# A gated linear attention and a routed MLP: the attention's instructions put in order by a list of operations with times

## The chip, the core and the metric

One core of a Trainium2 chip runs the program. Its engines work side by side and meet through semaphores: TensorE (PE, matmuls; PEld its weight loads), VectorE (DVE), ScalarE (ACT), GpSimd (POOL), and SyncE (SP), whose queue issues the DMAs here. The metric is the device time of one execution in microseconds; lower is better.

## The reference

The attention is a recurrence over 768 tokens for 4 batches of 8 heads of width 48; its output rows go to a mixture of 8 experts, one expert a row.

```python
mag = np.sqrt(a_re * a_re + a_im * a_im)
scale = np.minimum(mag, 0.999) / (mag + 1e-06)
a_re_n, a_im_n = (a_re * scale, a_im * scale)
...
for t in range(S):
    ar, ai = (a_re_n[:, :, t, :, None], a_im_n[:, :, t, :, None])
    new_re = ar * S_re - ai * S_im
    new_im = ar * S_im + ai * S_re
    kv = np.einsum('bhd,bhe->bhde', k[:, :, t], v[:, :, t])
    S_re, S_im = (new_re + kv, new_im)
    y[:, :, t] = np.einsum('bhd,bhde->bhe', q[:, :, t], S_re)
...
logits = x @ w_gate
expert_idx = np.argmax(logits, axis=1)
...
for e in range(E):
    mask = expert_idx == e
    xe = x[mask]
    h = np.maximum(xe @ w1[e], 0.0)
    ye = h @ w2[e]
    out[mask] = gate_w[mask, None] * ye
```

All inputs are float32: q, k, v and both gate parts are (4, 8, 768, 48); w1 is (8, 384, 1024), w2 (8, 1024, 384).

## The kernel before

The program has three parts in a row: the attention of the four batches, a short routing part, and 31 row tiles of the experts' MLP. The change touches the attention alone.

**What VectorE does for a batch (`front`).** Tokens are cut into 48 blocks of 16, and channels lie on partitions. `limit` turns the raw gates into a scale, in four pieces: per piece ScalarE squares, takes a logarithm, an exponential, a square and one affine pass with a bias held in a tile (`u<-l,w_bias`), and VectorE does four passes over 576 columns (`s<-sq`, `s<-s,u`, `l<-s,l`, `sc<-l,u`). The scaled gates are written into X (`X<-raw,sc`), which holds three parts per position: the negated imaginary part (ScalarE writes it), the real and the imaginary part. A chain over the 15 further positions of a block multiplies the gates up (`z<-X`, 576 columns, then `X<-z`, 288 columns). Small steps of 72 and 36 columns carry the products across blocks (`zc`, `carry`). `fix(t)` then brings the carried products into a third t of the channels (six passes of 672 columns), and `fold(t)` makes q times the product and k over the product (eight passes of 768 columns), into tiles called `pk`. SP ships `pk` to per-head tiles KX and QX by DMAs, for q and k, real and imaginary parts, one per piece of a head. Six KX/QX pairs serve the eight heads of a batch in turn; `pk` has three buffers.

**What the attention does for a group of heads (`attention`).** The groups of a batch have 2, 3 and 3 heads; their tokens come in six chunks of 128. In each chunk TensorE makes scores (`at<-QX,KX`), VectorE masks them (`am<-at,causal`), TensorE adds the masked scores times the values and the state times the queries into `y`, ScalarE moves `y` to `xf`; for the next chunk TensorE makes the turned state (`sp`) and ScalarE copies it to `st`. The scores' matmul is 224 columns wide, since QX holds a rotation matrix beside each chunk's queries: VectorE builds it for five chunks of a head at once (`QX<-diag,KX`, 96x480), and ScalarE copies the turned keys out (`kt<-at`). In the last group of a batch each finished chunk of 128 rows is transposed (`px`), copied (`xt`), multiplied with the gate weights (`lg`) and stored to `x_hbm`.

**What sets the order.** The instructions of VectorE, ScalarE and TensorE keep the order in which the Python code issues them (`InOrder`). `front` and `attention` are generators. `front` yields a guess of VectorE's time after each step; a group's `attention` generator is put on the list `waiting` with a start time (`spent[0] + SHIP`, 4.0), and `heads_until` takes steps from it as long as its own clock `spent[1]` is not ahead of `front`'s. `limit` of the next batch is drawn into the chain one step at a time from the seventh position on. The tiles come from rotating pools.

Of the kernel before, what the change touches and what calls it, by code (L numbers as in the profile page):

```python
# [21 lines left out]
BL = 16  # L22
# [7 lines left out]
SHIP = 4.0  # L30
# [8 lines left out]
def segments(t):  # L39

    r, out = t * 128, []
    while r < t * 128 + 128:
        n = min(D - r % D, t * 128 + 128 - r)
        out.append((r // D, r - t * 128, n, r % D))
        r += n
    return out
# [14 lines left out]
def gateloop_then_moe(ctx, tc, q, k, a_re, a_im, v, wg, w1, w2, out):  # L61
# [60 lines left out]
    with ExitStack() as att:  # L122
        pool = lambda nm, n, **kw: att.enter_context(tc.tile_pool(name=nm, bufs=n, **kw))
        ld = pool("ld", 2)
        one = pool("one", 1)
        two = pool("two", 2)
        sm = pool("sm", 3)
        psA = pool("psA", 4, space=PSUM)
        psY = pool("psY", 1, space=PSUM)
        psS = pool("psS", 1, space=PSUM)  # L130
        psX = pool("psX", 1, space=PSUM)
        psL = pool("psL", 1, space=PSUM)
        V, A, T = (InOrder(tc, e) for e in (nc.vector, nc.scalar, nc.tensor))
# [7 lines left out]


        KXs = [one.tile([128, KW], FP32, name=f"KX{i}") for i in range(RING)]
        QXs = [one.tile([128, C, 256], FP32, name=f"QX{i}") for i in range(RING)]
        KTs = [one.tile([128, 3, 128], FP32, name=f"kt{i}") for i in range(2)]
# [6 lines left out]
        X = one.tile([128, BL, 3, NC], FP32, name="X")  # L152
        xf = one.tile([128, C, DM], FP32, name="xf")
        turn, taken = [0], set()

        def load(b):
            raws = []
            for i in range(BL // JQ):
                js = slice(i * JQ, i * JQ + JQ)
                raw = ld.tile([128, JQ, 2, NC], FP32, name="raw", bufs=BL // JQ)  # L160
                nc.sync.dma_start(raw[:, :, 0, :], a_re[b, :, js, :])
                nc.sync.dma_start(raw[:, :, 1, :], a_im[b, :, js, :])
                raws.append(raw)
            return raws

        def limit(b, raws, scales):

            held, sqs = {}, {}

            def squares(i):  # L170
                if i < BL // JQ:
                    sq = two.tile([128, BL, 2, C * NB], FP32, name="sq").rearrange("p j u n -> p (j u n)")[:, 0:JQ * 2 * NC]
                    sqs[i] = sq.rearrange("p (j u n) -> p j u n", u=2, n=NC)
                    A.activation(sqs[i], raws[i], func=ACT.Square)
            squares(0)
            for i in range(BL // JQ + 2):
                if i < BL // JQ:
                    s = two.tile([128, JQ, NC], FP32, name="s")
                    sq = sqs.pop(i)
                    vstt(s, sq[:, :, 0, :], 1e-12, sq[:, :, 1, :], ALU.max, ALU.add)  # L180
                    yield
                if i >= 2:

                    _, l, u = held.pop(i - 2)
                    sc = two.tile([128, JQ, NC], FP32, name="sc", bufs=BL // JQ)
                    vstt(sc, l, -2 / 0.999, u, ALU.max, ALU.mult)
                    scales.append(sc)
                    yield
                if i < BL // JQ:
                    l, u = (two.tile([128, JQ, NC], FP32, name=x) for x in "lu")  # L190
                    A.activation(l, s, func=ACT.Ln)
                    A.activation(l, l, func=ACT.Exp, scale=-0.5)
                    A.activation(u, l, func=ACT.Square, accum_out=good[:, b, G * C + i:G * C + i + 1])
                    held[i] = s, l, u
                    squares(i + 1)
                if 1 <= i <= BL // JQ:

                    s1, l, u = held[i - 1]
                    vtt(s1, s1, u, ALU.mult)
                    yield  # L200
                    vstt(l, s1, -3.0, l, ALU.add, ALU.mult)
                    A.activation(u, l, func=ACT.Identity, scale=-0.5e-6 * 0.4995, bias=w_bias)
                    yield

        def front(b, raws, scales, heads, ahead):

            for i in range(BL // JQ):
                js = slice(i * JQ, i * JQ + JQ)
                vtt(X[:, js, 1:3, :], raws[i], bc(scales[i][:, :, None, :], [128, JQ, 2, NC]), ALU.mult)
                A.activation(X[:, js, 0, :], X[:, js, 2, :], func=ACT.Copy, scale=-1.0)  # L210
                yield 1.3
            raws[:] = load(b + 1) if b + 1 < B else []
            more = limit(b + 1, raws, ahead) if b + 1 < B else iter(())
            qs, ks = [], []
            for t in range(G):
                for x, src in ((qs, q), (ks, k)):
                    x.append(ld.tile([128, BL, C * NB], FP32, name="qt" if x is qs else "kt_in", bufs=1))
                    nc.sync.dma_start(x[t], src[b, :, t])

            for j in range(1, BL):  # L220
                cur, prev = X[:, j], X[:, j - 1]
                z = two.tile([128, 2, 2, NC], FP32, name="z")
                vtt(z, dims(cur, 0, (NC, 2), (NC, 2), (1, NC)), dims(prev, 2 * NC, (-NC, 2), (0, 2), (1, NC)), ALU.mult)
                if j > 6:
                    next(more, None)
                vtt(cur[:, 1:3, :], z[:, 0], z[:, 1], ALU.add)
                if j > 6:
                    next(more, None)
                yield 2.4 if j > 6 else 1.3
            for _ in more:  # L230
                pass

            last = one.tile([128, 3, NC], FP32, name="last")
            V.tensor_copy(last[:, 1:3, :], X[:, BL - 1, 1:3, :])
            V.tensor_scalar_mul(last[:, 0, :], X[:, BL - 1, 2, :], -1.0)
            carry = one.tile([128, 2, G * C, NB], FP32, name="carry")
            lv = last.rearrange("p u (n b) -> p u n b", b=NB)
            V.tensor_copy(carry[:, :, :, 1], lv[:, 1:3, :, 0])
            yield 0.7
            for n in range(2, NB):  # L240
                z = two.tile([128, 2, 2, G * C], FP32, name="zc")
                vtt(z, dims(last, n - 1, (NC, 2), (NC, 2), (NB, G * C)),
                    dims(carry, NC + n - 1, (-NC, 2), (0, 2), (NB, G * C)), ALU.mult)
                vtt(carry[:, :, :, n], z[:, 0], z[:, 1], ALU.add)
                yield 0.6
            TC = C * NB

            def fix(t):
                ts = slice(t * TC, t * TC + TC)
                xv = X[:, :, :, ts].rearrange("p j u (n b) -> p j u n b", b=NB)[:, :, :, :, 1:]  # L250
                shape = [128, BL, C, NB - 1]
                y = {}
                for x, w, nm in ((0, 0, "s"), (1, 1, "l"), (0, 1, "u"), (1, 0, "u")):
                    y[x, w] = two.tile([128, BL * TC], FP32, name=nm)[:, 0:BL * C * (NB - 1)]
                    y[x, w] = y[x, w].rearrange("p (j n b) -> p j n b", j=BL, b=NB - 1)
                    vtt(y[x, w], xv[:, :, 1 + x], bc(carry[:, w:w + 1, t * C:t * C + C, 1:], shape), ALU.mult)
                    yield 0.77
                vtt(xv[:, :, 1], y[0, 0], y[1, 1], ALU.subtract)
                yield 0.77
                vtt(xv[:, :, 2], y[0, 1], y[1, 0], ALU.add)  # L260
                yield 0.77

            def fold(t):
                ts = slice(t * TC, t * TC + TC)
                sq = two.tile([128, BL, 2, TC], FP32, name="sq")
                s, l = (two.tile([128, BL, TC], FP32, name=x) for x in "sl")
                A.activation(sq, X[:, :, 1:3, ts], func=ACT.Square)
                qp = two.tile([128, 2, KW], FP32, name="pk", bufs=3)
                kp = two.tile([128, 2, KW], FP32, name="pk", bufs=3)
                by_chunk = lambda ap: ap.rearrange("p j (c n) -> p c j n", n=NB)  # L270
                chunks = lambda ap: ap.rearrange("p (c j n) -> p c j n", j=BL, n=NB)
                pu = [by_chunk(X[:, :, 1 + u, ts]) for u in range(2)]
# [158 lines left out]
        def heads_until(now):  # L431
            while waiting and spent[1] <= now:
                ready, gen = waiting[0]
                spent[1] = max(spent[1], ready)
                if spent[1] > now:
                    break
# [320 lines left out]
```

## Time and profile before

| what | us |
|---|---|
| median of 3 runs (lowest, highest) | 882.89 (880.92, 884.51) |
| the profiled execution's own time | 885.0 |
| its span in the trace | 883.3 |
| busy: PE, DVE, ACT, POOL | 621.0, 422.3, 218.3, 138.0 |

The span counts from the first to the last instruction in the trace; stretches below are given in microseconds from its start. The chain that ended last holds only the last stores of the MLP, so it tells nothing of the attention. The attention is therefore read from the busy time of stretches and from the instructions in order of time: the stretches are cut where a batch's first mask (`am`) starts and where its last one starts.

### The profile page before, as it was taken

The page shows a single profiled execution, that of the slowest core. Times are in us where ns is not written, and L with a number is a line of the kernel's source. Part 1 is how long each engine was busy: PE and PEld are TensorE (multiplying, and loading weights), DVE is VectorE, ACT ScalarE, POOL GpSimd, SP SyncE. Part 2 cuts the span into 40 slices and gives each one's busy share as a digit, 9 for nine tenths or more (in the row PEclk, how much of TensorE's full clock was granted, in tenths as well). Part 3 has the DMA queues.
Part 4 walks back from the last instruction along what each step waited for, and adds up shares of the span by engine and source line. Part 5 has one row for each costly group of instructions (what it writes and reads, how often), then busy time and mean ns, then how long its engine had stood idle before and what let it go on. Part 6 is the DMA issues. An engine that isn't in the chain of part 4 may idle for free. (4 is left out here: it accounts for less than half of the span.)

```text
span 883.3 us, 10745 instructions
## 1 busy us (share of the span) xinstructions
PE 621.0 (70%) x3985; PEld 534.7 (61%) x3985; DVE 422.3 (48%) x760; ACT 218.3 (25%) x538; POOL 138.0 (16%) x160
## 2 busy tenths in 40 slices
PE   0000558926689167963599149999999999999997
PEld 0000557925679157962599047777777777777775
DVE  4889767896878958778631521111111111111111
ACT  5462236632356324332333100000000000000000
POOL 6000000000000000000000032333333333333320
PEclk9999978967879677985799659999999999999999
DMA  7302455235532444135221167787888798878850
GB/s 197 107 1 53 121 128 128 71 98 136 132 104 81 118 121 111 37 86 143 68 64 46 12 243 311 315 316 311 343 318 303 300 367 335 306 299 342 315 197 1
DMA packets 67627, 156.47 MB, mean 177 GB/s; under 512 B 9873, under 2 KB 50866, under 8 KB 59634
## 3 DMA queue, kind: packets, MB, share of 16 engines
q0 software_dynamic: 12896, 108.36, 32.0%
q1 hardware_dynamic: 51474, 47.36, 20.4%
q8 instruction: 33, 0.54, 0.2%
q10 hardware_dynamic: 3200, 0.01, 0.2%
q14 instruction: 24, 0.20, 0.1%
HBM read 127.23 MB, written 10.83 MB: 156 GB/s over the span
## 5 line engine op out<-in xcount | busy, mean ns | idle before, releaser
L57 PE MATMUL at<-QX,KX 128*128 128x224 f32 (+1 forms) x384 | 92.3, 382 | 165.9 <-DVE QX L57 165.9
L704 PEld LDWEIGHTS h_ps<-xt,w1t 128*128 128x128 f32 x1488 | 173.5, 194 | 12.7 <-issue 4.8
L57 PEld LDWEIGHTS at<-QX,KX 128*128 128x128 f32 x384 | 73.4, 215 | 171.2 <-issue 98.1
L704 PE MATMUL h_ps<-xt,w1t 128*128 128x128 f32 x1488 | 173.8, 277 | 4.4 <-issue 4.4
L710 PE MATMUL o_ps<-w2t,ht 128*128 128x384 f32 x496 | 167.9, 492 | 8.5 <-ACT ht L706 8.2
L710 PEld LDWEIGHTS o_ps<-w2t,ht 128*128 128x128 f32 x496 | 91.7, 190 | 71.9 <-ACT ht L706 14.4
L57 PE MATMUL y<-vb,am 128*128 128x128 f32 x384 | 78.3, 298 | 42.9 <-ACT xf L57 42.9
L706 ACT ACTIVATE ht<-h_ps 128x512 f32<-128x512 f32 x31 | 18.5, 598 | 357.0 <-PE h_ps L704 357.0
L57 PEld LDWEIGHTS y<-vb,am 128*128 128x128 f32 x384 | 67.1, 212 | 44.6 <-ACT xf L57 44.1
L712 DVE TENSOR_SCALAR yo<-o_ps,xs 128x384 f32<-128x384 f32 x31 | 19.2, 618 | 143.6 <-PE o_ps L710 143.6
L699 DVE COPY xt<-xt_ps 128x384 f32<-128x384 f32 x31 | 17.3, 557 | 139.8 <-PE xt_ps L697 139.8
L474 POOL MEMSET state<- 128x1152 f32 x1 | 1.1, 1063 | 472.6 <-DMA x_hbm<-xf 472.6
L57 PE MATMUL y<-st,QX 128*128 128x128 f32 x320 | 67.4, 294 | 3.4 <-ACT st L57 2.9
L57 DVE TENSOR_TENSOR am<-at,causal 128x256 f32<-128x256 f32 x120 | 41.1, 368 | 52.5 <-PE at L57 52.4
L57 PE MATMUL sp<-vb,kt 128*128 128x128 f32 x320 | 62.0, 288 | 0.0
L713 POOL DMA_INDIRECT out_dram<-yo,idx x31 | 31.5, 1016 | 194.0 <-DVE yo L712 193.1
L57 PEld LDWEIGHTS y<-st,QX 128*128 128x128 f32 x320 | 52.2, 205 | 6.6 <-ACT st L57 6.6
L57 PE MATMUL sp<-st,QX 128*128 128x128 f32 x256 | 52.7, 289 | 0.0
L57 ACT COPY kt<-at 128x192 f32<-128x192 f32 (+1 forms) x100 | 25.5, 288 | 102.3 <-DVE am L57 102.3
L57 PEld LDWEIGHTS sp<-vb,kt 128*128 128x128 f32 x320 | 50.6, 206 | 0.0
L57 DVE TENSOR_TENSOR z<-X 128x576 f32<-128x576 f32 x60 | 45.1, 752 | 0.7
L57 PEld LDWEIGHTS sp<-st,QX 128*128 128x128 f32 x256 | 40.8, 201 | 0.0
(142 smaller groups left out, 718.0 us busy)
## 6 DMA issues: line engine op xcount, KB each, us to landing
KX<-pk SPq DMA_DIRECT2D x48, 146.2 KB, 3.3
QX<-pk SPq DMA_DIRECT2D x48, 144.0 KB, 3.5
raw<-in_a_re_dram SPq DMA_DIRECT2D x16, 288.0 KB, 4.6
raw<-in_a_im_dram SPq DMA_DIRECT2D x16, 288.0 KB, 5.2
qt<-in_q_dram SPq DMA_DIRECT2D x12, 384.0 KB, 3.8
kt_in<-in_k_dram SPq DMA_DIRECT2D x12, 384.0 KB, 3.2
vb<-in_v_dram SPq DMA_DIRECT2D x24, 192.0 KB, 3.0
x_hbm<-xf SPq DMA_DIRECT2D x24, 192.0 KB, 2.7
```

Of the source, the lines that this page charges most:

```text
L57: return lambda *a, **kw: self.tc.keep_in_program_order(f(*a, **kw))
L474: nc.gpsimd.memset(state, 0.0)
L699: nc.vector.tensor_copy(xt, xt_ps)
L704: nc.tensor.matmul(h_ps[:, f, :], lhsT=w1t[:, c:c + 128], rhs=xt[:, d, :], start=(d == 0), stop=(d == DT - 1))
L706: nc.scalar.activation(ht[:, 0:FT // 2, :], h_ps[:, 0:FT // 2, :], func=ACT.Relu)
L710: nc.tensor.matmul(o_ps, lhsT=ht[:, f, :], rhs=w2t[:, f * DM:f * DM + DM], start=(f == 0), stop=(f == FT - 1))
L712: nc.vector.tensor_scalar_mul(y, o_ps, xs[:, DM:W])
L713: nc.gpsimd.indirect_dma_start(out=out[:, :], out_offset=bass.IndirectOffsetOnAxis(ap=idx[:, j:j + 1], axis=0), in_=y, in_offset=None, bou ...
```

## The change

The attention is no longer issued as the code runs. Each step is put on a list as an `Op` with its engine (V, A, T or S for SP), the time that it keeps its engine, the time until others may use its result (`late`), the operations that it needs (`after`), those whose buffer it overwrites (`free`), and a rank (`first`). `in_time` then places the operations one by one at the earliest time of the four engines; among those that are ready on an engine it takes the lowest rank, then the one with the longest way to the end. The instructions are issued in that order, SP's DMAs too.

Beside the order:

- the gates are loaded into four fixed tiles `gate` of three parts and scaled in place; X keeps two parts. ScalarE copies position 0 to X, and makes `last` (VectorE did before);
- the rotation matrices are made by ScalarE, one 96x48 ACTIVATE for each half, chunk and head, with the factor from a column of KX (`diagonal`), where VectorE had one 96x480 pass for a head;
- all tiles of the attention are fixed buffers with their own names instead of pools' turns, and PSUM is eight fixed banks (`bank0` to `bank3` are the scores, then `y`, `sp`, `px`, `lg`);
- `zrow` stands in a small pool of its own, released before the `setup` tiles are made.

```diff
-SHIP = 4.0
...
+class Op:
+    def __init__(self, engine, busy, late, emit, after, free, first):
+        self.engine, self.busy, self.late, self.emit, self.first = engine, busy, late, emit, first
+        self.after, self.free = [o for o in after if o], [o for o in free if o]
+        self.start = None
+    def ready(self):
+        t = 0.0
+        for o in self.after:
+            t = max(t, o.start + o.late)
+        for o in self.free:
+            t = max(t, o.start + (o.busy if o.engine == self.engine else o.late))
+        return t
...
+def in_time(ops):
...
+    while len(out) < len(ops):
+        best = None
+        for e, l in able.items():
+            if l:
+                t = max(clock[e], min(x[0] for x in l))
+                if best is None or t < best[0]:
+                    best = t, e
+        t, e = best
+        r, o = min((x for x in able[e] if x[0] <= t), key=lambda x: (x[1].first, -way[x[1]]))
+        able[e].remove((r, o))
+        o.start, clock[e] = t, t + o.busy
...
-    zrow = consts.tile([1, W], FP32, name="zrow")
-    nc.vector.memset(zrow, 0.0)
-    nc.sync.dma_start(x_hbm[N:N + 1, :], zrow)
+    with tc.tile_pool(name="zero", bufs=1) as setup:
+        zrow = setup.tile([1, W], FP32, name="zrow")
+        nc.vector.memset(zrow, 0.0)
+        nc.sync.dma_start(x_hbm[N:N + 1, :], zrow)
...
+        def dve(cols, emit, after=(), free=(), first=5):
+            return op("V", cols / 960 + 0.068, cols / 960 + 0.19, emit, after, free, first)
+        def act(cols, emit, after=(), free=(), first=5, n=1):
+            return op("A", n * 0.08 + cols / 1200, n * 0.08 + cols / 1200 + 0.15, emit, after, free, first)
+        def pe(passes, emit, after=(), free=(), first=5):
+            return op("T", passes * 0.111, passes * 0.111 + 0.21, emit, after, free, first)
+        def dma(late, emit, after=(), free=()):
+            return op("S", 0.62, late, emit, after, free)
...
-                vtt(X[:, js, 1:3, :], raws[i], bc(scales[i][:, :, None, :], [128, JQ, 2, NC]), ALU.mult)
-                A.activation(X[:, js, 0, :], X[:, js, 2, :], func=ACT.Copy, scale=-1.0)
+                o = dve(2 * n, lambda g=g, s=s: vtt(g[:, :, 1:3, :], g[:, :, 1:3, :], bc(s[:, :, None, :], [128, JQ, 2, NC]), ALU.mult),
+                        [sc])
+                m = act(n, lambda g=g: A.activation(g[:, :, 0, :], g[:, :, 2, :], func=ACT.Copy, scale=-1.0), [o])
...
-            for i in range(n):
-                ends = KX[i][0:R2, S:KW].rearrange("p (c w) -> p c w", w=2)[:, 0:C - 1, :, None]
-                shape = [R2, C - 1, 2, D]
-                vtt(QX[i][0:R2, 0:C - 1, 128:128 + R2].rearrange("p c (w d) -> p c w d", w=2),
-                    bc(diag[:, None, :, :], shape), bc(ends, shape), ALU.mult)
+            for c in range(C - 1):
+                for i in range(n):
+                    def diagonal(i=i, c=c):
+                        for w in range(2):
+                            A.activation(QX[i][0:R2, c, 128 + w * D:128 + w * D + D], diag[:, w, :], func=ACT.Copy,
+                                         scale=KX[i][0:R2, S + 2 * c + w:S + 2 * c + w + 1])
+                    turn[c, i] = act(96, diagonal, kd[i], state.get(("head", slots[i]), []), first=2, n=2)
...
-        for b in range(B):
-            heads, ahead = {}, []
-            for x in front(b, raws, scales, heads, ahead):
-                if isinstance(x, tuple):
-                    waiting.append((spent[0] + SHIP, attention(b, x[0], heads)))
-                else:
-                    spent[0] += x
-                heads_until(spent[0])
+        load_gates(0)
+        limit(0)
+        for b in range(B):
+            front(b)
+            if b + 1 < B:
+                load_gates(b + 1)
+            fixed = [fix(t) for t in range(G)]
+            for t in range(G):
+                fold(b, t, fixed[t])
+                attention(b, t)
+            if b + 1 < B:
+                limit(b + 1)
+        for o in in_time(ops):
+            o.emit()
```

What moves, at three places. First VectorE, in the first batch, from the masks of the first group's third chunk on (`am` masks, `pk<-X,qt` and `pk<-X,l` or `pk<-X,fl` the products with q and k, `s`, `l` or `fs`, `fl` steps of `fold`). Before:

```order
L57 TENSOR_TENSOR am<-at,causal 128x256
L57 TENSOR_TENSOR pk<-X,l 128x768 x2
L57 TENSOR_TENSOR pk<-X,qt 128x768
L57 TENSOR_TENSOR am<-at,causal 128x256
L57 SCALAR_TENSOR_TENSOR s<-sq 128x768
L57 TENSOR_TENSOR pk<-X,qt 128x768
L57 TENSOR_SCALAR good<-s 128x6
L57 TENSOR_TENSOR am<-at,causal 128x256
```

Behind the products with k of the second third, the product with q of the last third stands ahead of the next mask. The same place in the changed kernel:

```order
L110 TENSOR_TENSOR am_186<-bank_194,causal 128x256
L110 TENSOR_TENSOR pk_174<-X,qt 128x768
L110 TENSOR_TENSOR am_187<-bank_195,causal 128x256
L110 TENSOR_TENSOR pk_172<-X,fl 128x768
L110 TENSOR_TENSOR am_184<-bank_192,causal 128x256
L110 TENSOR_TENSOR pk_172<-X,fl 128x768
L110 SCALAR_TENSOR_TENSOR fs<-fsq 128x768
L110 TENSOR_TENSOR ls_161<-ls_161,lu_163 128x576
L110 TENSOR_SCALAR good<-fs 128x6
L110 SCALAR_TENSOR_TENSOR ll_162<-ls_161,ll_162 128x576
L110 TENSOR_TENSOR am_185<-bank_193,causal 128x256
```

All six masks of the group now stand ahead (two of them just above these rows) of the last third's product with q, between single passes of `fold` and of the next batch's `limit`.

Second ScalarE, in the first batch's first group and the step to the second. Before:

```order
L57 ACTIVATE xf<-y 128x96
L57 COPY st<-sp 128x256
L57 ACTIVATE sq<-X 128x1536
L57 COPY pk<-X 128x6
L57 ACTIVATE pk<-X 128x6
L57 COPY kt_142<-at 128x2x96
L57 ACTIVATE l<-s 128x768
L57 ACTIVATE l<-l 128x768
```

After, in the same place:

```order
L110 ACTIVATE xf<-bank_196 128x96
L110 COPY st_188<-bank_197 128x256
L110 ACTIVATE QX_121<-diag,KX_115 96x48 x4
L110 ACTIVATE xf<-bank_196 128x96
L110 ACTIVATE QX_122<-diag,KX_116 96x48 x4
L110 ACTIVATE QX_121<-diag,KX_115 96x48 x2
L110 ACTIVATE QX_122<-diag,KX_116 96x48 x2
```

The rotation matrices of the next group's heads now stand among the copies that TensorE waits for.

Third GpSimd, at the start of the program, with the semaphores that a row waits on (a name with DMAHW is a DMA's; `tok_i`, `pos_i` and `diag_i` feed the masks' constants). Before:

```order
L95 IOTA tok_i 128x128
masks.py:199 AFFINE_SELECT ident<-ident 128x128 [waits Pool_49]
L99 IOTA pos_i 128x3
L108 IOTA diag_i 96x96
L147 MEMSET KX_130 32x780 [waits Pool_49]
```

After:

```order
masks.py:199 AFFINE_SELECT ident<-ident 128x128 [waits Pool_49]
L149 IOTA tok_i 128x128 [waits DMAHW1_49,DVE_49]
L153 IOTA pos_i 128x3
L162 IOTA diag_i 96x96
L196 MEMSET KX_113 32x780 [waits DVE_49,Pool_49]
```

`tok_i` now waits for a DMA, the store of `zrow`, and the two iotas behind it with it.

## Rows read from the trace of the kernel before

**Rows 1.** Busy us by stretch: from:to length, PE PEld DVE ACT POOL, PEclk, DMA, GB/s.

```profile
9.98:99.78 89.80, 2.21 (x5) 1.58 (x6) 71.07 (x112) 40.12 (x65) 6.45 (x10) 1.00 0.36 97
...
207.76:282.51 74.75, 60.30 (x406) 57.85 (x406) 57.85 (x101) 39.05 (x102) 0.00 (x0) 0.87 0.40 105
282.51:315.12 32.61, 9.52 (x67) 8.31 (x66) 28.30 (x50) 9.63 (x25) 0.00 (x0) 0.65 0.47 127
315.12:382.49 67.37, 57.11 (x406) 55.09 (x406) 47.86 (x84) 24.07 (x78) 0.00 (x0) 0.89 0.32 81
...
414.97:488.05 73.08, 62.67 (x466) 61.37 (x465) 27.73 (x53) 24.36 (x83) 0.00 (x0) 0.90 0.25 61
488.05:883.30 395.25, 349.07 (x2106) 275.78 (x2105) 71.66 (x155) 20.37 (x34) 122.57 (x131) 0.95 0.72 275
```

**Rows 2.** Order of time, VectorE, then TensorE: start, us, instruction, [idle before <-releaser].

```profile
223.90 0.96 DVE L57 TENSOR_TENSOR pk<-X,qt 128x768 f32<-128x768 f32 x1 [6.91 <-DMA KX<-pk]
...
228.00 0.80 PE L57 MATMUL y<-vb,am 128*128 128x128 f32 x2 [9.08 <-ACT xf L57]
...
255.83 0.79 PE L57 MATMUL y<-vb,am 128*128 128x128 f32 x2 [3.42 <-ACT xf L57]
```

**Rows 3.** Order of time, VectorE: neighbours' starts, and three rotation matrices in a row.

```profile
61.33 0.75 DVE L57 SCALAR_TENSOR_TENSOR l<-s,l 128x576 f32<-128x576 f32 x1
61.99 0.75 DVE L57 TENSOR_TENSOR z<-X 128x576 f32<-128x576 f32 x1
...
123.39 1.78 DVE L57 TENSOR_TENSOR QX<-diag,KX 96x480 f32<-96x480 f32 x3
...
306.69 0.95 DVE L57 SCALAR_TENSOR_TENSOR s<-sq 128x768 f32<-128x768 f32 x1
307.56 0.95 DVE L57 TENSOR_TENSOR pk<-X,qt 128x768 f32<-128x768 f32 x1
```

**Rows 4.** Order of time, TensorE: scores at the head of a chunk or a group.

```profile
259.38 4.85 PE L57 MATMUL at<-QX,KX 128*128 128x224 f32 x12 [0.63 <-DVE QX L57]
...
440.73 2.44 PE L57 MATMUL at<-QX,KX 128*128 128x224 f32 x12
...
444.34 1.30 PE L57 MATMUL at<-QX,KX 128*128 128x224 f32 x6
...
448.15 1.30 PE L57 MATMUL at<-QX,KX 128*128 128x224 f32 x6
...
469.89 1.30 PE L57 MATMUL at<-QX,KX 128*128 128x224 f32 x6
...
474.70 1.30 PE L57 MATMUL at<-QX,KX 128*128 128x224 f32 x6
```

**Rows 5.** Groups by line and shape, ScalarE, up to 490 us; then order of time.

```profile
L57 ACT ACTIVATE u<-l,w_bias 128x576 f32<-128x576 f32 x16 | 12.3, 768 | 6.2 <-DVE l L57 6.1
...
L57 ACT ACTIVATE u<-l 128x576 f32<-128x576 f32 x16 | 11.0, 685 | 0.5
...
L57 ACT ACTIVATE xf<-y 128x48 f32<-128x48 f32 x72 | 10.0, 213 | 15.5 <-PE y L57 15.4
...
172.56 0.42 ACT L57 ACTIVATE xf<-y 128x48 f32<-128x48 f32 x3 [0.53 <-PE y L57]
```

**Rows 6.** The program's start: GpSimd and SP in order of time; SP's waits; x_hbm's landings.

```profile
1.07 0.27 POOL L95 IOTA tok_i<- 128x128 int32 x1
...
1.36 0.32 SPq L87 DMA_DIRECT2D x_hbm<-zrow  x1
4.72 0.42 SPq L161 DMA_DIRECT2D raw<-in_a_re_dram  x1
...
SPq L161 <- DVE diag L72: 3.0, 1, 3.0
...
DMA to landing us min/median/max: 2.1/3.0/14.4
```

**Rows 7.** Order of time, VectorE: the first third's products with k, third batch.

```profile
304.07 1.83 DVE L57 TENSOR_TENSOR pk<-X,l 128x768 f32<-128x768 f32 x2
```

More of the change, by code (lines that the diff above doesn't have):

```diff
@@ L45, in segments, with let @@
         r += n
+    return out
+class Op:
[11 more added lines that the diff above has]
+def in_time(ops):
+    users, left, way = {}, {}, {}
+    for o in ops:
+        left[o] = len(o.after) + len(o.free)
+        for p in o.after + o.free:
+            users.setdefault(p, []).append(o)
+    for o in reversed(ops):
+        way[o] = o.late + max((way[u] for u in users.get(o, ())), default=0.0)
+    able, clock, out = {e: [] for e in "VATS"}, dict.fromkeys("VATS", 0.0), []
+    def let(o):
+        able[o.engine].append((o.ready(), o))
+    for o in ops:
+        if not left[o]:
+            let(o)
+    while len(out) < len(ops):
[9 more added lines that the diff above has]
+        o.start, clock[e] = t, t + o.busy
+        out.append(o)
+        for u in users.get(o, ()):
+            left[u] -= 1
+            if not left[u]:
+                let(u)
     return out
@@ L151, in gateloop_then_moe @@
             nc.gpsimd.memset(KTs[i][:, :, R2:], 0.0)
[L152 to L157, printed above, removed]
+        gates = [buf(f"gate{i}", JQ, 3, NC) for i in range(BL // JQ)]
+        X = buf("X", BL, 2, NC)
+        zs = [buf(f"z{i}", 2, 2, NC) for i in range(2)]
+        last, carry, zc = buf("last", 3, NC), buf("carry", 2, G * C, NB), [buf(f"zc{i}", 2, 2, G * C) for i in range(2)]
@@ new lines, in gateloop_then_moe, with op @@
+        sts = [buf(f"st{i}", 3, 128) for i in range(2)]
+        xts = [buf(f"xt{i}", DT, 128) for i in range(2)]
+        ps = [bank.tile([128, 512], FP32, name=f"bank{i}") for i in range(8)]
+        ats = [p.rearrange("p (h w) -> p h w", w=256) for p in ps[0:4]]
+        y_ps, sp_ps, px_ps = (p[:, 0:384].rearrange("p (h w) -> p h w", w=128) for p in ps[4:7])
+        lg_ps = ps[7][:, 0:C * E].rearrange("p (c e) -> p c e", e=E)
+        ops, used = [], {}
+        def op(engine, busy, late, emit, after=(), free=(), first=0):
+            ops.append(Op(engine, busy, late, emit, list(after), list(free), first))
+            return ops[-1]
@@ L162, in load @@
[L162 to L203, printed above, removed]
@@ L421, in attention @@
-            if late:
-                logits(*late)
-                yield 0.7
-            taken.difference_update(slots)
-            if g == G - 1:
-                A.copy(lg_all[:, b * C:(b + 1) * C, :], lgs[0])
-        values, lgs, spent, waiting = [], [], [0.0, 0.0], []
[L431 to L436, printed above, removed]
-                took = next(gen, None)
-                if took is None:
-                    waiting.pop(0)
-                else:
-                    spent[1] += took
@@ L443, in gateloop_then_moe @@
[L443 to L455 removed]
+                    (w, readers), (wa, am_readers) = ring("at", 4), ring("am", 4)
@@ new lines, in attention, with score @@
+                    at, a = ats[w], ams[wa]
+                    def score(r=r, at=at, c=c, wide=wide):
+                        for i in r:
+                            T.matmul(at[:, i % 2, 0:wide], lhsT=KX[i][:, c * 128:c * 128 + 128], rhs=QX[i][:, c, 0:wide],
+                                     start=True, stop=True)
+                    o = pe(len(r) * (3.4 if c < C - 1 else 2), score, sum((qd[i] + kd[i] + [turn.get((c, i))] for i in r), []), readers,
+                           first=rank)
```

426 lines of the change are left out of this document (228 added, 198 removed).

## The prediction, made before the changed kernel was run

> **What bounds the kernel now.** I cut the span into stretches and read the busy time of each [rows 1]. The routing and the MLP take 395 us behind 488.05 and are the same instructions in both kernels, so the question is when the attention ends. It has a head, up to the first mask of batch 0 at 99.78; then for each batch a *window*, first mask to last mask (74.75 us in the second batch), and a *gap*, last mask to the next batch's first (32.61); in the last batch, first mask to the end (73.08). The first window and the two gaps left out are within 0.5 us of the rows shown. The sum is 99.78 + 74.92 + 33.06 + 74.75 + 32.61 + 67.37 + 32.48 + 73.08 = 488.05.
>
> In a gap VectorE is busy 28.30 of 32.61 us and TensorE 9.52: VectorE sets it. In a window neither is full: VectorE 57.85, TensorE 60.30, ScalarE 39.05 of 74.75. The loss sits in single waits. VectorE's product with q of the last third waits 6.91 us for a DMA from a `pk` tile (one such wait stands in each window, four in all); it has a mask queued behind it, so TensorE stands 9.08 us; another 3.42 us follows [rows 2]. After such a stop TensorE runs at its low level: twelve score matmuls take 4.85 us behind it and 2.44 us where it had been busy [rows 4]; the windows' granted clock is 0.87 and 0.89 [rows 1].
>
> **The change, part by part.**
>
> *The start.* `tok_i` began at 1.07 and now waits for the store of `zrow`, which is issued at 1.36; landings of that tensor take 2.1 us at the least [rows 6]. So it starts at about 3.7, 2.6 us later; `diag` hangs on it, and the first gate load waits for `diag` (3.0 us, issued at 4.72) [rows 6]. Loss: +2.6 us, bounds 2 and 4. Nothing hides it: VectorE and ScalarE wait for those gates.
>
> *VectorE's work.* Independent passes in a row start 0.66 us apart for 576 columns and 0.87 us for 768 [rows 3], so about 0.07 us plus 1.04 ns a column; with that every row of the order can be priced. One rotation matrix of 480 columns is 0.57 us (three in a row end after 1.78 [rows 3]); eight a batch, 4.6 us, leave VectorE, and so do the two `last` copies, 0.6 us. The scaling in place costs what the scaling into X cost. By rows times spacings a window and a gap together held 81.4 us and now hold 76.2 (the difference is those 5.2). What moves is larger: the new window has 45.9 us (30 masks 8.4, the chain 15.5, twelve `limit` passes 8.0, three gate scalings 3.8, `fold` 9.6, the rest 0.6), the gap 30.3 (18 `fix` passes 13.8, 13 `fold` passes 11.3, four `limit` passes and one scaling 3.9, carries 1.2). In batch 2, which has little `limit` behind it, 43.2 and 18.2, because seven `fix` passes and all carries moved into the window.
>
> *The pack wait.* In the new order the last third's product with q stands behind the group's six masks, and its `pk` tile was last read by the first third's k DMAs, issued before the window began. I take the 6.9 us as gone. What is late next is TensorE itself.
>
> *TensorE's work* is unchanged. A chunk of three heads takes 3.81 us at the high level and 4.81 us in the last group [rows 4]; two heads, two thirds of 3.81, 2.54. Six chunks of each are 67.0 us; the first and last chunk of a group lack the state matmuls, about 1.04 us a head, 8.3 for eight heads. So 59 us a batch, and in the new order the last score stands 11 us before the end of its list: a window needs 48 us of TensorE at the high level. Each window begins after some 20 us of a nearly idle TensorE, so its first matmuls run low, as they do now; 12 score matmuls cost 2.4 us more that way [rows 4], I take 3. For waits on `st` and masks inside a window I take 4 us; the bound below is 0, above 12 (then the window is as long as the third one of now, 67.4, in which VectorE had slack and no `limit` work stood among the masks [rows 1]). Window: 48 + 3 + 4 = 55, bounds 49 and 67. VectorE's 45.9 fits under it.
>
> *ScalarE's work.* 320 small ACTIVATEs are added, 80 a batch, 60 of them in the window. A 48-column pass costs (0.42 - 0.21) / 2 = 0.10 us in a row, and an operand from a tile costs 768 - 685 = 83 ns [rows 5], so about 0.18 us each; the planner counts 0.12. That puts 60 x 0.18 = 11 us on the window's 39 [rows 1]: 50 of 55. It is covered, but thinly: ScalarE is in order, and behind a rotation matrix that waits for its KX DMA stands the `st` copy that TensorE waits for. So I allow for it inside the 4 us of waits. The Trainium skill ("ScalarE: Activation LUTs", "What ACT_TABLE_LOAD costs") gives 186 ns plus 0.833 ns a column, 93 ns for a pointer operand and an overlap of 93 ns, which would be an estimate of 226 ns for each of these; it speaks against moving ten short passes in for one 480-column pass on VectorE. By it the window's load is 52 to 53 us and the sum some 8 us higher; the 83 ns row is close to its 93.
>
> *The gap.* VectorE's 30.3 us, plus what dependent small steps and the shipping add. Now 25.6 us by the same spacings took 32.6, 7 more. From the end of the first third's products with k (304.07 + 1.83) to the first mask at 315.12 are 9.2 us [rows 1, 7]; in the new order 8.2 us of VectorE's work stands between, so about 1.5 us is open, and the carries have other passes between them. I take 30.3 + 4.2 = 34.5, bounds 33 and 37; behind batch 2, 18.2 + 3.8 = 22, bounds 20 and 25.
>
> *The head.* Now 9.98 us to the first pass, then 65.8 us of spacings in 89.8 us [rows 1]: 24 us are lost, 11 of them before the chain, where `limit` runs alone. Now the chain starts on the first piece while the others are still in `limit`; ScalarE's first results still bound the first 8 us (4 us lost), and I allow 5.5 us for the rest. But more is drawn in: 71.3 us stand ahead of the first mask, three pieces of the next `limit` among them. 10.0 + 2.6 + 71.3 + 9.5 = 93.4, bounds 88 and 100.
>
> *The end.* From the first mask of the last batch: 59 us of TensorE, 2 low (its stop is shorter), 4 of waits: 65 against 73.08; bounds 61 and 71. VectorE has 19.7 us there.
>
> Sum: 93.4 + 55 + 34.5 + 55 + 34.5 + 55 + 22 + 65 = 414.4 against 488.05: 73.7 us less. Against the profiled execution's 885.0 that is 811.3; the median of the runs, 882.89, lies 2 us below it, so I say **810**.
>
> **The rivals.**
>
> *Windows stay long.* The plan's prices are those of a TensorE at the high level and of a quick ScalarE; where one is late, three engines in fixed order wait together. If the windows are 67.4 (what one takes now with VectorE at slack) and the end 71: 3 x 12.4 + 6 = 43 more, **853**. For it: ScalarE at 50 of 55. Against it: all copies that TensorE needs were ranked by these very chains.
>
> *Tight windows.* If VectorE's 45.9 and TensorE's 48 overlap without waits, windows 50, head 90, end 62: 21 less, **789**.
>
> *The clock falls (slower than before).* Place: TensorE in the windows. Its work is priced at 2.4 GHz; at 1.2 GHz each us of it takes two. It decides when 73.7 of the 4 x 59 = 236 us of attention matmuls, 31%, run low beyond the 3 us a window already counted. At half low the time is 811 + 118 - 11 = **918**. For it: after stops of 9.08 and 3.42 us it ran low [rows 2, 4]. Against it: the stops that did it are those removed, and the present windows are granted 0.87 to 0.89 with 14 us of stops in them [rows 1]. The Trainium skill ("TensorE: Matmul & The Clock Gate", "What's actually happening") says that the low level is the default and activity lifts it; by that rule a plan of many short waits could hold the low level, and the trace so far shows it only behind stops such as these.
>
> *Nothing comes of it*: the planner's order leaves the windows at 74 and only head and rotation matrices change, 6 + 5 us less, about **875 to 885**.
>
> **How the numbers follow.** Forecast (796 to 830) 0.61; long windows 0.16; tight windows 0.12; clock 0.06; nothing 0.05. The range reaches from 786, into the tight case, to 848, most of the way to the long one; that leaves out about 0.2. A measurement can tell about 0.5% from no change, 4.4 us; all cases but the clock and half of the last are faster by more: faster 0.90, same 0.04, slower 0.06.
>
> **What would show it.** In the changed profile: the first gate load at about 7.3; the first mask near 93; no DVE wait of over 3 us on a `pk` DMA; windows of 50 to 60 us with a granted clock of 0.9 or more; gaps of 33 to 37 us in which VectorE is nearly full; ScalarE's QX<-diag at about 0.18 us apart. Wrong if windows pass 67, if TensorE waits long for `st` copies behind rotation matrices, or if the clock in the windows is below 0.84.

## The result, and the profile after

The changed kernel takes 806.3 us (803.7 to 806.9), the kernel before in the same set of runs 883.1: a ratio of 0.913 with an interval of 0.910 to 0.915, 8.7% faster. The forecast was 810, within 786 to 848. The profiled execution spans 804.7 us.

The stretches of [rows 1] as the changed kernel has them, cut in the same way (first mask of a batch, last mask of a batch, end of the attention): busy us by stretch, from:to length, PE PEld DVE ACT POOL, PEclk, DMA, GB/s. (The first row starts at 10.00; VectorE's first pass starts at 9.70.)

```profile
10.00:90.50 80.50, 2.21 (x5) 1.59 (x6) 73.57 (x114) 44.78 (x84) 8.80 (x14) 1.00 0.38 100
90.50:145.91 55.41, 51.53 (x381) 49.63 (x381) 48.07 (x91) 45.64 (x160) 0.00 (x0) 1.00 0.57 146
145.91:179.64 33.73, 13.29 (x92) 12.14 (x92) 31.26 (x49) 18.79 (x52) 0.00 (x0) 0.65 0.47 113
179.64:234.98 55.34, 51.45 (x381) 49.54 (x381) 48.18 (x91) 45.61 (x160) 0.00 (x0) 0.97 0.55 147
234.98:269.03 34.05, 13.60 (x92) 12.45 (x92) 31.35 (x51) 18.80 (x52) 0.00 (x0) 0.64 0.47 113
269.03:326.23 57.20, 53.31 (x387) 51.30 (x387) 47.06 (x95) 36.94 (x142) 0.00 (x0) 0.94 0.41 103
326.23:345.94 19.71, 12.14 (x87) 10.87 (x86) 18.53 (x27) 12.45 (x39) 0.00 (x0) 0.77 0.67 171
345.94:409.50 63.56, 60.54 (x466) 58.71 (x465) 21.82 (x44) 38.59 (x154) 0.00 (x0) 0.98 0.32 82
409.50:804.70 395.20, 349.32 (x2106) 275.92 (x2105) 71.52 (x155) 20.36 (x34) 122.73 (x131) 0.95 0.72 275
```

The reader is to see three things. The last row is what it was (395.25 before): all the gain is in the attention, which ends at 409.50 and not at 488.05. The windows went from 67 to 75 us down to 55 to 57, with TensorE busy for 51 to 53 of them, at a granted clock of 0.94 to 1.00 where it was 0.87 to 0.89. The two long gaps became no shorter, and VectorE fills them as before.

The 1.00 of the first window is not to be taken at its word. Behind the first two score matmuls, fourteen follow in the first batch, then in the second:

```profile
89.38 5.45 PE L110 MATMUL bank<-QX,KX 128*128 128x224 f32 x14 [0.26 <-issue]
...
178.49 5.28 PE L110 MATMUL bank<-QX,KX 128*128 128x224 f32 x14 [0.23 <-ACT QX L110]
```

Both run at the low level (twelve take 2.44 us at the high one [rows 4]), although the record of the clock has 1.00 for the first place and 0.50 for the second.

What each engine waits for in the second window: instruction, releaser, us in all, times, longest. TensorE first, then VectorE.

```profile
PE bank L110 <- ACT xf L110: 1.9, 2, 1.3
PE bank L110 <- ACT kt L110: 1.4, 1, 1.4
PE bank L110 <- ACT QX L110: 0.6, 1, 0.6
...
DVE am L110 <- PE bank L110: 5.7, 8, 2.3
DVE am L110 <- ACT st L110: 1.7, 1, 1.7
DVE ls L110 <- ACT lsq L110: 1.3, 1, 1.3
```

No wait for a `pk` DMA is left, and TensorE's longest stop fell from 9.08 us [rows 2] to 1.4. Its 3.9 us of stops all end at ScalarE: at copies (`xf`, `kt`) or at a rotation matrix.

### The profile page after: what moved, and what is told of

Read it like the earlier page. It is cut to its first block, busy times and chain, and to the rows that moved or that the text cites. A ratio compares the mean times of both kernels' runs of the same rounds, so it can differ in the third digit from the quotient of the medians.

```text
span 804.7 us, 11063 instructions
## 1 busy us (share of the span) xinstructions
PE 607.4 (75%) x3985; PEld 522.1 (65%) x3985; DVE 393.3 (49%) x720; ACT 284.4 (35%) x870; POOL 138.1 (17%) x160
## 5 line engine op out<-in xcount | busy, mean ns | idle before, releaser
L110 PE MATMUL bank<-QX,KX 128*128 128x224 f32 (+1 forms) x384 | 90.5, 378 | 135.4 <-DVE fl L110 88.0
L110 PEld LDWEIGHTS bank<-QX,KX 128*128 128x128 f32 x384 | 72.1, 212 | 142.3 <-issue 88.8
L110 PE MATMUL bank<-st,QX 128*128 128x128 f32 x576 | 107.1, 276 | 1.5 <-ACT st L110 1.5
L110 PEld LDWEIGHTS bank<-st,QX 128*128 128x128 f32 x576 | 86.2, 192 | 2.2 <-ACT st L110 1.9
L110 ACT ACTIVATE QX<-diag,KX 96x48 f32<-96x48 f32 x320 | 77.1, 327 | 19.0 <-DMA KX<-pk 19.0
L110 PE MATMUL bank<-vb,am 128*128 128x128 f32 x384 | 72.7, 279 | 7.1 <-ACT xf L110 7.0
L110 DVE TENSOR_TENSOR am<-bank,causal 128x256 f32<-128x256 f32 (+1 forms) x120 | 42.5, 367 | 62.3 <-PE bank L110 56.5
L110 PEld LDWEIGHTS bank<-vb,am 128*128 128x128 f32 x384 | 58.2, 192 | 9.8 <-ACT xf L110 9.6
L110 PE MATMUL bank<-vb,kt 128*128 128x128 f32 x320 | 59.2, 278 | 0.0
L110 PEld LDWEIGHTS bank<-vb,kt 128*128 128x128 f32 x320 | 48.0, 195 | 0.1
```

The lines of the kernel that those rows point to most:

```text
L110: return lambda *a, **kw: self.tc.keep_in_program_order(f(*a, **kw))
```

## Experiments

Ratios are to the kernel before in the same set of runs; medians of different sets differ by up to 0.7% for that same kernel.

**1. The `pk` wait alone.** The kernel before, with room made for a fourth buffer (the edits that make the room are left out here):

```diff
...
-                qp = two.tile([128, 2, KW], FP32, name="pk", bufs=3)
-                kp = two.tile([128, 2, KW], FP32, name="pk", bufs=3)
+                qp = two.tile([128, 2, KW], FP32, name="pk", bufs=4)
+                kp = two.tile([128, 2, KW], FP32, name="pk", bufs=4)
...
```

> The kernel before with a fourth `pk` buffer (room for it by a single `xt`, single `sq` tiles and `zrow` in a pool of its own), order untouched. If the wait for `pk` is by itself what stretched the old windows, the 6.9 us on VectorE and the 9.08 us stop of TensorE behind it go from each of four windows: 28 to 36 us less than before, 847 to 855, windows of 66 to 68. If the wait was only the place where an order without times happened to meet, another wait stands there and the time stays within 875 to 885.

Measured: 855.3 us, ratio 0.968 (0.966 to 0.971), 28 us less. Its second batch, window and gap:

```profile
201.18:267.30 66.12, 57.27 (x406) 53.79 (x406) 57.59 (x100) 38.85 (x102) 0.00 (x0) 0.95 0.43 118
267.30:299.79 32.49, 9.52 (x67) 8.32 (x66) 28.30 (x50) 9.61 (x25) 0.00 (x0) 0.63 0.48 127
```

The window of 74.75 us became 66.12, at a clock of 0.95: that wait is 28 of the 77 us, and its clock loss goes with it. The other 49 lie elsewhere: beside this kernel the changed one has 10 us less in the head (first mask at 100.75 and 90.50), 23 less in the first two windows and 12 less in the gap behind batch 2. What the fixed buffers and the gates scaled in place give by themselves was not tried.

This kernel also has `zrow` in a pool of its own. Its `tok_i` starts at 2.66 and its first gate load is issued at

```profile
6.00 0.43 SPq L162 DMA_DIRECT2D raw<-in_a_re_dram  x1
```

which is 1.3 us later than the 4.72 of before. Its first mask is 1.0 us later with it (100.75 and 99.78), so the wait itself is worth some 29 us.

**2. The rotation matrices alone.** The kernel before, with them on ScalarE, a group's all ahead of its scores:

```diff
...
-                vtt(QX[i][0:R2, 0:C - 1, 128:128 + R2].rearrange("p c (w d) -> p c w d", w=2),
-                    bc(diag[:, None, :, :], shape), bc(ends, shape), ALU.mult)
...
+                    for w in range(2):
+                        A.activation(QX[i][0:R2, c, 128 + w * D:128 + w * D + D], diag[:, w, :], func=ACT.Copy,
+                                     scale=KX[i][0:R2, S + 2 * c + w:S + 2 * c + w + 1])
```

> The kernel before with the rotation matrices on ScalarE, all of a group's ahead of its first scores as its code issues them, nothing else. If moving them off VectorE is a large part of the gain, 8 x 0.57 us go from VectorE in each of four batches: 18 us less, about 865. If the gain is the planner's and the matrices only pay when they are spread, a group's 20 or 30 passes at 0.225 us, 4.5 to 6.8 us, stand ahead of its first scores and of the copies that TensorE waits for: no gain or a loss, 880 to 905.

Measured: 925.8 us, ratio 1.048 (1.045 to 1.051): 42 us slower. Its second window, and in order of time a start late in it on TensorE, with the idle time before, and what stood ahead of it on ScalarE:

```profile
219.57:306.24 86.67, 63.15 (x406) 58.69 (x406) 57.04 (x103) 53.84 (x173) 0.00 (x0) 0.86 0.35 90
```

```profile
287.56 1.65 PE L57 MATMUL sp<-vb,kt 128*128 128x128 f32 x6 [6.75 <-ACT kt L57]
...
276.64 6.85 ACT L57 ACTIVATE QX<-diag,KX 96x48 f32<-96x48 f32 x30
...
287.21 0.80 ACT L57 COPY kt<-at 128x192 f32<-128x192 f32 x4
```

ScalarE is busy 53.84 of 86.67 us, so it is not short of time: the `kt` copy stands behind 30 rotation passes of the next group and then 3.8 us of `limit` passes, and TensorE stands 6.75 us for it. Here the delay comes from what stands ahead on an engine that works in order, not from its load.

**3. The matrices back on VectorE, in the planner's order.**

```diff
...
-                    turn[c, i] = act(96, diagonal, kd[i], state.get(("head", slots[i]), []), first=2, n=2)
...
+                o = dve(480, diagonal, kd[i], state.get(("head", slots[i]), []), first=2)
+                for c in range(C - 1):
+                    turn[c, i] = o
```

> The changed kernel with the rotation matrices back on VectorE, one 96x480 pass for a head, put in order by the same planner. If VectorE sets the gaps and has 7 us free in a window, as the forecast has it, 1.1 us come into each gap and 3.4 into each window, part of them covered: 2 to 18 us slower than the changed kernel, 808 to 824, I say 814. If ScalarE in order is what still stretches the windows (TensorE waits 2.6 us in each behind rotation matrices), taking 60 short passes out of each gives back more than VectorE loses: 795 to 804.

Measured: 800.0 us, ratio 0.907 (0.904 to 0.910), against 0.913 for the changed kernel: faster by some 6 us, the rival's side. Second batch:

```profile
178.73:232.62 53.89, 52.20 (x403) 50.78 (x401) 50.84 (x97) 31.09 (x92) 0.00 (x0) 0.99 0.60 161
232.62:266.97 34.35, 12.87 (x71) 12.16 (x70) 32.24 (x53) 16.99 (x38) 0.00 (x0) 0.57 0.39 94
```

VectorE does 83.1 us of work in window and gap instead of 79.5, and the two together still take 88.2 instead of 89.4: the changed kernel did not use what it had taken off VectorE.

**4. Each rotation matrix made twice** on ScalarE (`for w in (0, 1, 0, 1)`), in the changed kernel's order.

> The changed kernel with each rotation matrix made twice over, the planner's prices untouched. 60 more passes at 0.225 us, 13.5 us, come on ScalarE's 45.6 of 55.4 us in a window: 59. If the cover on ScalarE is as thin as the forecast has it, windows grow to 60 to 65 and the time to 822 to 845. If ScalarE is far from setting the windows they stay within 2 us and the time within 806 to 814.

Measured: 886.7 us, ratio 1.003: the whole gain gone, 80 us and not the 15 to 40 expected. Second window:

```profile
201.96:274.83 72.87, 56.43 (x381) 53.73 (x381) 48.55 (x91) 61.62 (x232) 0.00 (x0) 0.88 0.40 104
```

TensorE's waits in it, as above:

```profile
PE bank L110 <- ACT xf L110: 8.2, 3, 4.8
PE bank L110 <- ACT kt L110: 4.2, 2, 3.2
PE bank L110 <- ACT QX L110: 4.0, 2, 3.8
```

ScalarE is busy 61.62 of 72.87 us, again not full. Both theories were too mild: passes that the plan does not know of delay the copies behind them, TensorE stands 16.4 us at ScalarE where it stood 3.9, VectorE's masks wait for TensorE 17.0 us where they waited 5.7, and the clock falls to 0.88.

**5. One price for all.** `dve`, `act` and `pe` all give 0.6 us busy, 0.8 until the result may be used.

```diff
...
-            return op("V", cols / 960 + 0.068, cols / 960 + 0.19, emit, after, free, first)
+            return op("V", 0.6, 0.8, emit, after, free, first)
...
```

> The changed kernel with one price in the planner for every operation of VectorE, ScalarE and TensorE (0.6 us busy, 0.8 until others may use it); list, needs, ranks and buffers as they are. If the times are what makes the order good, single engines are planned far from what they do (a mask 0.28 to 0.42, a product 0.87, ten matmuls 2 us): windows of 60 to 75, 820 to 870. If needs and ranks alone make the order, windows stay within 3 us and the time within 803 to 814.

Measured: 910.9 us, ratio 1.031 (1.029 to 1.034). With the same list, needs, ranks and buffers the time is longer than with the hand-written order. VectorE's waits for TensorE, from the first mask on (in the changed kernel 56.5 us over the whole attention):

```profile
DVE am L110 <- PE bank L110: 132.6, 84, 7.7
```

The numbers in the price functions are needed for the gain: without them it is gone, and 28 us more. Only this one flat price was tried.

**6. The right price of a rotation pass.** In order of time on ScalarE of the changed kernel, passes in a row:

```profile
103.53 1.01 ACT L110 ACTIVATE QX<-diag,KX 96x48 f32<-96x48 f32 x4
...
107.41 2.81 ACT L110 ACTIVATE QX<-diag,KX 96x48 f32<-96x48 f32 x12
```

Eight more take (2.81 - 1.01) / 8 = 0.225 us each; the planner counted 0.12.

```diff
-                    turn[c, i] = act(96, diagonal, kd[i], state.get(("head", slots[i]), []), first=2, n=2)
+                    turn[c, i] = act(96, diagonal, kd[i], state.get(("head", slots[i]), []), first=2, n=4.6)
```

> The changed kernel with the planner told 0.22 us for one rotation pass on ScalarE instead of 0.12. Putting the matrices back on VectorE gave 6.3 us. If that came from a plan that counted ScalarE too cheap, the right price gives most of it: 799 to 803. If it is the work itself, which no order can hide on an engine that the copies for TensorE also need, the time stays at 804 to 809.

Measured: 794.9 us, ratio 0.900 (0.899 to 0.902): 11 us less than the changed kernel by one number, with the same instructions, and 5 less than with the matrices on VectorE. What TensorE waited for at ScalarE between 90 and 400 us, changed kernel first (the 43.0 and 50.8 us for `QX` are almost all the stops ahead of the windows), then with the right price:

```profile
PE bank L110 <- ACT QX L110: 43.0, 9, 17.4
PE bank L110 <- ACT xt L110: 7.0, 5, 1.8
PE bank L110 <- ACT xf L110: 7.0, 8, 1.3
PE bank L110 <- ACT kt L110: 4.1, 3, 1.4
PE bank L110 <- ACT st L110: 1.5, 2, 1.1
```

```profile
PE bank L110 <- ACT QX L110: 50.8, 4, 34.4
PE bank L110 <- ACT xt L110: 4.0, 5, 1.1
PE bank L110 <- ACT xf L110: 0.9, 2, 0.6
...
PE bank L110 <- ACT st L110: 0.2, 1, 0.2
```

The waits for copies went from 19.6 to 5.1 us. The second window has TensorE busy from end to end:

```profile
162.80:211.69 48.89, 48.85 (x378) 48.47 (x378) 42.30 (x75) 45.58 (x161) 0.00 (x0) 0.99 0.58 147
```

ScalarE does as much in it as before (45.58 us, 45.61 in the changed kernel), so most of the loss behind ScalarE was the order and not the amount of its work. Two things stay open. The order moved everywhere: the four windows together lost 18 us, while the three gaps (20.2, 50.6 and 24.4 us) gained 8. And only this one other price was tried, so a gain from another order by chance is not told apart from a gain from the right price; experiment 9 finds 9 us by another change of the order.

**7. `zrow` back among the constants**, as before the change, in one execution.

```diff
-    with tc.tile_pool(name="zero", bufs=1) as setup:
-        zrow = setup.tile([1, W], FP32, name="zrow")
+    zrow = consts.tile([1, W], FP32, name="zrow")
...
```

> The changed kernel with `zrow` back among the constants, as before; one look at the start. `tok_i` then starts at about 1.1 again. If what held the first gate load at 4.72 before was VectorE's small passes running slow beside GpSimd's memsets, and the memsets wait for `diag` here, VectorE's passes take their 0.15 to 0.3 us and the first gate load is issued at 2.6 to 3.0. If it was only the iotas' time, it is issued at 4.4 to 4.7 again.

Measured: the first gate load at 2.98 us, the first mask at 89.64, 804.2 us. The start of three kernels in order of time, GpSimd's memsets beside VectorE's small passes and SP's first gate load: before, then changed, then this one.

```profile
1.92 0.74 POOL L147 MEMSET KX<- 32x780 f32 x1
2.60 1.45 POOL L148 MEMSET QX<- 32x1536 f32 x1
...
1.90 0.83 DVE L111 CAST diag_f<-diag_i 96x96 f32<-96x96 int32 x1
...
2.76 1.36 DVE L113 TENSOR_SCALAR diag<-diag_f 96x96 f32<-96x96 f32 x1
```

```profile
4.44 0.74 POOL L196 MEMSET KX<- 32x780 f32 x1 [1.16 <-DVE diag L125]
...
3.33 0.20 DVE L165 CAST diag_f<-diag_i 96x96 f32<-96x96 int32 x1
...
4.41 0.43 SPq L110 DMA_DIRECT2D gate<-in_a_re_dram  x1
```

```profile
3.02 0.74 POOL L195 MEMSET KX<- 32x780 f32 x1 [1.16 <-DVE diag L125]
...
1.89 0.21 DVE L164 CAST diag_f<-diag_i 96x96 f32<-96x96 int32 x1
...
2.98 0.42 SPq L110 DMA_DIRECT2D gate<-in_a_re_dram  x1
```

With the iotas where they were before, the first gate load still comes 1.7 us sooner, so the iotas had not held it at 4.72 [rows 6]. What differs is that the memsets now wait for `diag`: beside one, the cast took 0.83 us and not 0.21, and a later pass 1.36, and each ended 0.07 us behind the memset's end.

**8. TensorE kept at its high level.** The kernel of experiment 3, with matmuls that nobody reads in the stops ahead of the first three windows: by the edit and the trace 62 in each stop, and not the 52 of the expectation below.

```diff
+        def warm(tile_ap, after, n):
+            def emit():
+                for _ in range(n):
+                    o = ps[7][:, 128:224].rearrange("p (u n) -> p u n", u=2) if len(tile_ap.shape) == 3 else ps[7][:, 128:256]
+                    T.matmul(o, lhsT=ident, rhs=tile_ap, start=True, stop=True)
+            return pe(2 * n, emit, after, first=-1)
...
+                rq += [warm(qp[:, u, 0:128], [prod[u]], 8) for u in range(2)]
+                rk += [warm(kp[:, u, 0:128], [kprod[u]], 8) for u in range(2)]
...
```

> The kernel with the matrices on VectorE, and in the stops of TensorE ahead of the first three windows 52 matmuls whose results nobody reads, spread over the last 15 us before the first scores. If the low level behind such a stop costs what the forecast has it (3 us, the first twelve score matmuls 4.06 instead of 2.44), those take 2.4 to 2.8 us and three windows lose 1.5 to 3 us each: 792 to 796. If VectorE and not TensorE sets the end of a window, or the matmuls in the stop hold up the first scores, the time is 798 to 804.

Measured: 802.2 us, ratio 0.908 (0.907 to 0.910), no gain over experiment 3. The second batch's first scores, in order of time, then its window and gap:

```profile
178.49 2.44 PE L110 MATMUL bank<-QX,KX 128*128 128x224 f32 x12
```

```profile
180.04:230.50 50.46, 49.10 (x377) 47.19 (x376) 47.64 (x92) 29.63 (x89) 0.00 (x0) 1.00 0.63 159
230.50:269.50 39.00, 30.90 (x224) 30.28 (x222) 35.44 (x57) 18.72 (x41) 0.00 (x0) 0.78 0.39 100
```

The scores ran at the high level (2.44 us, as [rows 4] have it behind a busy TensorE), the window is 3.4 us shorter than in experiment 3, and the gap 4.7 longer: window and gap together do not shrink (89.5 and 88.2), with VectorE busy 83.1 us in both. From the first mask of the attention to its last it is 305.4 us here and 305.5 in experiment 3, so the higher level gained nothing there. The 2 us lost lie ahead of it. The first batch's scores, here and in experiment 3:

```profile
90.13 2.44 PE L110 MATMUL bank<-QX,KX 128*128 128x224 f32 x12
```

```profile
88.32 4.82 PE L110 MATMUL bank<-QX,KX 128*128 128x224 f32 x12 [88.32 <-DVE QX L110]
```

Here they start 1.8 us later, right behind the extra matmuls, and the first mask comes at 92.25 instead of 90.45; the second batch's scores are late by as much (178.49 and 176.56).

**9. The ranks left out.**

```diff
-        r, o = min((x for x in able[e] if x[0] <= t), key=lambda x: (x[1].first, -way[x[1]]))
+        r, o = min((x for x in able[e] if x[0] <= t), key=lambda x: -way[x[1]])
```

> The changed kernel with the planner's ranks left out of its choice: among the ready operations of an engine the one with the longest way to the end, alone. If the ranks (masks and `st` copies first) keep TensorE fed, windows lengthen by 2 to 8 us each and the time goes to 812 to 835. If times and longest ways already put them there, 802 to 810.

Measured: 797.3 us, ratio 0.899 (0.896 to 0.901): faster than the changed kernel, which neither theory had. What TensorE waited for between 90 and 400 us, the row with the longest stop of all:

```profile
PE bank L110 <- DVE am L110: 11.5, 7, 3.3
```

The long stops between the batches are gone: in this order the batches follow each other on TensorE without the 17 us ahead of a window. Which of the ranks had held that back was not tried.

**10 to 12. Together.** Right price and `zrow` as before; the same with the last groups' matrices on VectorE; that one without ranks.

> The same without the VectorE passes: all matrices on ScalarE at the right price, `zrow` back. If the earlier start reaches the end it is 1 to 3 us under the 794.9 of the right price alone: 792 to 794; if it is lost on the way, 795.

> The planner told 0.22 us for a rotation pass on ScalarE, `zrow` back among the constants, and the matrices of the last group of each batch as one VectorE pass a head. If the two engines share the matrices better than either alone, 30 short passes fewer stand on ScalarE in each window against 1.7 us more on VectorE: 786 to 792. If VectorE, which sets a window and a gap together, pays all of that, 4 x 1.7 us: 798 to 803.

> The mixed kernel (right price, last groups' matrices on VectorE, `zrow` among the constants) with the ranks left out of the planner's choice too. Leaving the ranks out gave 9 us with the low price. If that gain and the 11 us of the right price are the same one (ScalarE's copies behind too many rotation passes), it is 0.890 to 0.900 of the time before, as the mixed kernel alone. If the ranks held VectorE's chain back by themselves, the gains add: under 0.888.

Measured: 798.6, 794.6 and 795.8 us, beside 886.7, 886.7 and 888.9 of the kernel before: ratios 0.899 (0.896 to 0.901), 0.895 (0.893 to 0.898) and 0.894 (0.893 to 0.896). The kernel before was slower in these sets, so the ratios are to be compared and not the times. The earlier start is lost within the interval (0.900 without it). The mixed form is the fastest, about 2% faster than the changed kernel, and 0.895 of 883.6 is 791, inside its first range; but it leads the right price alone by half a per cent only, with an interval that overlaps that of 0.899. Leaving the ranks out adds nothing there, which agrees with both cures being for the same trouble and does not show it.

## Why the prediction was right, point by point

- **The stretches.** Forecast against measured: head 93.4 and 90.5; windows 55 each and 55.4, 55.3, 57.2; gaps 34.5 and 33.7, 34.1; the one behind batch 2 22 and 19.7; the end 65 and 63.6. The errors add to -4.9 us, which is 414.4 against 409.5. (The first window of the kernel before ends at its last mask at 175.7 and not at 174.70; that moves 0.9 us from its gap to the window, and the sum is the same.)
- **The start was wrong.** The step said `tok_i` moves to 3.7 and the first gate load 2.6 us with it. `tok_i` came at 2.75 and the gate load at 4.41, 0.3 us sooner than before. The wait is there, but both terms behind it were too large. `tok_i` started 1.39 us after the store was issued, where the step took the 2.1 us of [rows 6] as the least. And the step kept the old time from `tok_i` to the gate load, which was 3.65 us, with VectorE's passes standing beside memsets, where the changed kernel needs 1.66 (experiment 7). Where the memsets do not wait for `diag`, a loss does come, 1.3 us (experiment 1). In the sum all of the head's error is this: VectorE's first `limit` pass came at 9.70 and not at 12.6, and the 80.8 us behind it are those of the forecast (71.3 + 9.5).
- **The pack wait** went, as the step on it said, and without it alone the kernel before is 28 us shorter (experiment 1).
- **TensorE's terms** came out in sum: 48 us at the high level and 3 low against 51.45 busy, 4 of waits against 3.9 in the second window. How the 51.45 divide between the two levels is not shown, beyond the fourteen low matmuls at the start. The 2.2 us more in the third window lie in the busy time (53.31), not in the waits (3.9). The rival of a falling clock did not come: 0.97 and 0.94 in the second and third window. Where the order was disturbed it stayed or fell back to what it was before (0.88 in experiment 4, 0.86 in experiment 2), and in experiment 2 the six `sp` matmuls behind the stop of 6.75 us ran low. The Trainium skill ("TensorE: Matmul & The Clock Gate", "What's actually happening") has activity lift the level, which agrees with the 2.44 us of the scores and the 1.00 in a window that experiment 8 entered busy; the time did not follow there.
- **ScalarE's price was the term that was mis-sized**: 0.18 us taken, 0.225 measured. The Trainium skill ("ScalarE: Activation LUTs", "What ACT_TABLE_LOAD costs") leads to 0.226 as an estimate; the trace agrees with it, and the sum from [rows 5] was low; which of its two parts was, no run shows. The load did not follow the price: ScalarE was busy 45.6 us of the second window and not 50, because other work left the window (three pieces of `limit` instead of four, no `xt` copies). The 52 to 53 us that the forecast worked out from the Trainium skill did not come either. So two errors met in this term, and that the 4 us of waits held is in part luck. What the step missed is that the planner's 0.12 was not only a matter of load but an error in the order; with the price put right the kernel is 11 us faster (experiment 6).
- **The 4.6 us a batch that leave VectorE** were counted as a gain in window and gap. Experiment 3 puts them back and is faster: as planned here the move cost some 6 us. It gained 5 only with the right price. So this part of the sum was not there, and the rest of the change gave more than the steps had it.
- **The gaps** are VectorE's, as forecast: 31.3 of 33.7 us busy. Experiment 8 bears it out: what the windows gave, the gaps took back.

## What to carry to other kernels

A planned order is as good as its prices: measure the spacing of each form in a trace, in a row and with the operands that it really has, before the plan is believed; here one number put right gave 11 us, and flat ones cost 105. On an engine that works in order, count for each moved instruction what stands behind it and who waits for that, not the engine's busy share, since ScalarE lengthened windows while it was 62 to 85% busy (experiments 2 and 4). When a start-up step is moved, look at what ran beside it in the old place before its old duration is carried over.

## What the hardware showed that was not expected

A cast of 96x96 on VectorE took 0.20 or 0.21 us alone and 0.83 beside a GpSimd memset of 0.74; a later pass took 1.36 beside the next, of 1.45, and 0.21 in the changed kernel. In the kernel of experiment 1 the same cast took 1.45 beside a memset of 1.37. In all three places the pass ended 0.07 us behind the memset. The Trainium skill ("SBUF — State Buffer", "Who interferes with whom") has GpSimd and a VectorE pass that runs in a mode with two ports, which a cast and a tensor_scalar can do, share a pair of ports: one of them holds it for a whole instruction while the other is blocked. The passes that end with the memset agree with it. Which of the two came first is not told here: both casts are listed as starting 0.01 or 0.02 us ahead of the memset that they ended with.
